# Two products exchanged at the end, and one half of a weighting moved from GpSimd to VectorE, in a one-core attention and FFN kernel

## The chip, the cores and the metric

One core of a Trainium2 chip runs the whole program. The metric is device time in microseconds of one execution. Between executions of the same program the times spread by one to two us (the eleven runs of the old kernel in one call took 342.58 to 344.05), so verdicts are made from several runs of each kernel on the same chip, in rounds that alternate the two. "Span" is the time from the first to the last instruction of the one execution that was profiled; it is some 1.7 us shorter than the device time. A run counts as fast when it is within 1.5% of the fastest of its kernel; only fast runs are compared.

## The reference, cut to what matters

```python
# performer attention, 8 batches x 8 heads x 576 positions x 64; 128 random features
phi(x) = exp(proj - sq - max) / sqrt(m)          # for q and k
kv  = einsum('bhsm,bhsd->bhmd', k_p, v);  z = sum_s k_p
out = (q_p @ kv) / (q_p @ z)
# then a gated FFN on 4608 tokens: 512 -> 1536 -> 512
g = x @ w_gate;  gelu = 0.5 * g * (1 + erf(g / sqrt(2)));  y = (gelu * (x @ w_val)) @ w_out
```

The kernel streams eight batches through attention and then, in blocks of 512 tokens, through the FFN. Two of the FFN's products are made in Strassen's way: seven block products in place of eight, with sums of blocks on VectorE and GpSimd.

## The kernel before: the parts that matter

The program's names, as far as they are needed: `wk` is the scale of k, `kz` the product of k's features with the weighted v, `nd` numerator and denominator of a batch, `pk` the projection of k; `val_one` and `val_two` are accumulators of the FFN's value product. The matmuls of this kernel write to tiles that it calls PSUM tiles (`out_one`, `kz_ps` and the like). In the profile PE is TensorE, DVE VectorE, ACT ScalarE, POOL GpSimd and SP the engine that in this kernel only issues DMAs and waits.

The weighting of v. Each half is one multiplication of 128x1152 elements and one small cast; the kz matmuls read them, the first half of kz only half 0, the second only half 1.

```python
def v(self, half, eng):
    ...
    isl = slice(half * NI // 2, (half + 1) * NI // 2)
    eng.tensor_mul(vev[:, isl, :, :D], vfv[:, isl],
                   wkv[:, isl].unsqueeze(3).broadcast_to((P, NI // 2, 2, D)))
    eng.tensor_copy(vev[:, isl, :, D], wkv[:, isl])
```

Its place in the start of the program (batch 0), in the order in which each engine gets its instructions:

```python
a.w()                       # wk = exp(nmax), ScalarE
a.qt.pe(0)
fill(12)
a.qf(1, True)
a.v(1, pool)                # second half on GpSimd
a.qt.copy(0, dve)
a.v(0, nc.vector)           # first half on VectorE
...
a.kz(0, False)              # reads half 0
a.kz(1)                     # reads half 1
n.qt.copy(0, dve)
n.qt.copy(1, dve)
a.kzc(dve)
```

The last row blocks. `pm` is one of the seven products (six matmuls), `pa` adds a PSUM tile to the output row, `pc` copies one, `pst` stores. Products 1, 6, 7 and 4 of a block are accumulated in one PSUM tile, `out_one`, and read out in between:

```python
def pm(self, s, n, i0, i1):
    ...
    ps = self.two[s][:, 0] if n in (3, 5) else self.two[s][:, 1] if n == 2 else self.one[s]
    for i in range(i0, i1):
        nc.tensor.matmul(ps, x[:, i, s * P:(s + 1) * P], y[:, i], start=n in (1, 2, 5) and i == 0, ...)

def store(c0, o_sb, ns=..., queues=(nc.sync, nc.sync)):
    for i in range(2):      # two DMAs of 64 rows each
        queues[i].dma_start(out=..., in_=o_sb[i * SP:(i + 1) * SP, :])
```

One wait is put in by hand: the DMA transposes of k of batch 2 are held until the load of v of batch 1 has landed.

```python
m = Attention(2)
behind(loads[-2], [m.by_dma("k")])
m.by_dma("q")
```

The softmax here doesn't subtract the row's maximum and nothing guards it: scores larger than these inputs give would overflow.

## Time and profile before

| what | value | from |
|---|---|---|
| device time, median of 3 | 343.06 us (342.66 to 343.08) | the timed runs |
| span of the profiled run | 341.0 us | the page |
| TensorE busy, granted clock | 96%, 0.998 | the page and the view of the cores |
| last copy of the output on VectorE ends | 337.65 us | the timeline |
| from there to the end | 3.3 us | 341.0 - 337.65 |

Reading it: TensorE (PE) is the bound nearly everywhere, so time can only come from the few gaps of PE on the chain, from the head before PE is full, and from the stretch after its last matmul. A timeline row gives start in us, duration in us, engine, line, operation, output and inputs; what stands in brackets at its end is the idle time of that engine ahead of it and what released it. The lines themselves are in the prediction below.

### The profile page before, as it was taken

The numbers are of one execution on the slowest core, as the hardware profiler recorded it, in microseconds if no ns is written. First come the engines' busy times: TensorE is split into PE (matmuls) and PEld (weight loads), VectorE is DVE, ScalarE is ACT, GpSimd is POOL, SyncE is SP. The second block draws the span as 40 slices with busy tenths as digits, with TensorE's granted clock in tenths as the row PEclk, the third lists the DMA queues.
The fourth block names the chain that finished last, engine by engine and source line by source line (L and its number), as shares of the span: only waits on it lengthen the run. The fifth ranks groups of instructions, "written<-read, shape, count | busy, mean of one in ns | idle before, by whom it ended". The sixth has DMA issues, their size and how long they took to land.

```text
span 341.0 us, 7993 instructions
## 1 busy us (share of the span) xinstructions
PE 327.4 (96%) x3114; PEld 206.0 (60%) x3155; DVE 229.1 (67%) x481; ACT 214.3 (63%) x434; POOL 149.9 (44%) x152
## 2 busy tenths in 40 slices
PE   7889999889999999999999999999999999999994
PEld 3565455566646664566447654665466786686683
DVE  3875388979773768375936683677457777796783
ACT  4894366774778558756875677658765447626640
POOL 8326004033486447744674559477968400000000
PEclk9999999999999999999999999999999999999999
DMA  8999999599889256945498629671413040013004
GB/s 155 275 206 207 206 272 206 137 174 236 178 135 331 49 102 91 326 89 108 60 326 113 116 32 291 164 111 19 94 33 63 8 115 11 1 32 93 2 0 124
DMA packets 67173, 45.08 MB, mean 132 GB/s; under 512 B 47296, under 2 KB 60096, under 8 KB 67136
## 3 DMA queue, kind: packets, MB, share of 16 engines
q0 software_dynamic: 14848, 22.12, 31.4%
q1 hardware_dynamic: 51744, 21.64, 30.4%
q10 hardware_dynamic: 544, 0.82, 0.8%
q8 instruction: 24, 0.39, 0.5%
q14 instruction: 13, 0.11, 0.1%
HBM read 37.78 MB, written 9.44 MB: 138 GB/s over the span
## 4 chain that ended last, share of the span: by engine, by line
PE 83%; DVE 6%; DMA 3%; ACT 3%; issue 2%; POOL 2%; DVEq 0%; POOLq 0%
PE g_ps L433 20%; PE o_ps L559 18%; PE val_one L378 11%; PE val_two L378 9%; PE out_one L533 5%; PE out_two L533 3%; PE v_ps L462 3%; PE g_ps L425 3%; PE kz_ps L285 3%; DMA q_in<-in_q_dram 2%; PE nd L302 2%; PE pk L220 2%; DVE x_sb L314 2%; PE pq L242 2%; DVE val_c L387 1%
## 5 line engine op out<-in xcount | busy, mean ns | idle before, releaser
L433 PE MATMUL g_ps<-xT,w_gate_sb 128*128 128x512 bf16 x352 | 108.2, 379 | 0.5
L440 ACT ACTIVATE g_gelu<-g_ps 128x512 bf16<-128x512 f32 x108 | 63.6, 598 | 54.1 <-PE g_ps L433 25.3
L559 PE MATMUL o_ps<-w_out_sb,gated 128*128 128x512 bf16 x275 | 64.6, 380 | 1.1 <-issue 0.6
L480 POOL TENSOR_TENSOR gated<-g_gelu,val_c 128x512 bf16<-128x512 bf16 x29 | 33.7, 1164 | 52.2 <-DVE iden L313 26.3
L387 DVE TENSOR_TENSOR val_c<-val_one,val_c 128x256 f32<-128x256 f32 x48 | 20.3, 424 | 49.0 <-ACT g_gelu L440 40.0
L378 PEld LDWEIGHTS <-w_val_sb 128*128 128x128 bf16 x384 | 36.5, 98 | 17.3 <-issue 1.4
L559 PEld LDWEIGHTS <-gated 128*128 128x128 bf16 x288 | 26.5, 98 | 33.5 <-issue 3.9
L383 ACT COPY val_c<-val_one 128x256 f32<-128x256 f32 x95 | 35.2, 371 | 11.2 <-PE val_one L378 8.1
L378 PEld LDWEIGHTS <-val_sums 128*128 128x128 bf16 x288 | 27.3, 98 | 24.4 <-DVE x_sb L314 3.7
L249 ACT ACTIVATE q_pT<-pq 128x512 bf16<-128x512 f32 (+1 forms) x68 | 34.6, 598 | 11.7 <-PE pq L242 11.5
L233 DVE TENSOR_REDUCE nmax<-pk 128x8 f32<-128x1024 f32 (+2 forms) x43 | 39.7, 968 | 2.9 <-PE pk L220 1.4
L433 PEld LDWEIGHTS <-w_gate_sb 128*128 128x128 bf16 x376 | 34.9, 98 | 11.2
L228 ACT ACTIVATE k_p<-pk 128x1024 bf16<-128x1024 f32 (+2 forms) x43 | 33.0, 832 | 8.1 <-PE pk L220 6.4
L378 PE MATMUL val_one<-x_sums,w_val_sb 128*128 128x256 bf16 x192 | 36.6, 272 | 0.6 <-DVE val_c L387 0.4
L387 DVE TENSOR_TENSOR val_c<-val_two,val_c 128x256 f32<-128x256 f32 x96 | 36.0, 414 | 0.8 <-PE val_two L378 0.7
L271 POOL TENSOR_TENSOR v_ext<-vf,wk 128x1152 bf16<-128x1152 f32 x12 | 28.2, 2347 | 13.9 <-ACT wk L260 13.9
L484 POOL TENSOR_TENSOR gated<-g_gelu,val_c 128x256 bf16<-128x256 bf16 x34 | 24.1, 711 | 15.0 <-ACT g_gelu L440 15.0
L314 DVE TENSOR_TENSOR x_sb<-nd,iden 128x512 bf16<-128x512 f32 (+2 forms) x41 | 27.8, 677 | 1.4
L564 DVE COPY o_sb<-o_ps 128x512 f32<-128x512 f32 x20 | 13.7, 685 | 19.4 <-PE o_ps L559 14.9
L383 ACT COPY val_c<-val_two 128x256 f32<-128x256 f32 x45 | 16.8, 373 | 11.7 <-PE val_two L378 11.7
L484 DVE TENSOR_TENSOR gated<-g_gelu,val_one 128x256 bf16<-128x256 bf16 x48 | 20.0, 416 | 6.0 <-ACT g_gelu L440 5.7
L378 PE MATMUL val_two<-x_sums,val_sums 128*128 128x256 bf16 x96 | 18.4, 274 | 1.0 <-POOL x_sums L455 0.3
(104 smaller groups left out, 486.3 us busy)
## 6 DMA issues: line engine op xcount, KB each, us to landing
out_dram<-o_sb SPq DMA_DIRECT2D x67, 128.0 KB, 3.3
vf<-in_v_dram POOLq DMA_DIRECT2D x7, 1152.0 KB, 12.4
q_in<-in_q_dram POOLq DMA_DIRECT2D x8, 576.0 KB, 9.4
k_in<-in_k_dram POOLq DMA_DIRECT2D x7, 576.0 KB, 6.2
w_gate_sb<-in_moe_w_gate_dram POOLq DMA_DIRECT2D x3, 512.0 KB, 17.7
w_val_sb<-in_moe_w_val_dram POOLq DMA_DIRECT2D x3, 512.0 KB, 19.4
w_out_sb<-in_moe_w_out_dram POOLq DMA_DIRECT2D x3, 512.0 KB, 13.4
vf<-in_v_dram SPq DMA_DIRECT2D x1, 1152.0 KB, 5.7
```

The lines of the kernel that those rows point to most:

```text
L228: last["begun"] = nc.scalar.activation(self.k_p[:, gs, i0:i0 + n, :], pk, func=Exp)
L233: nc.vector.reduce_max(self.nmax[:, gs, i0:i0 + n], pk, axis=AX, negate=True)
L249: last["begun"] = nc.scalar.activation(dst[:, a, i0:i0 + n], self.pq[c][a].rearrange("m (i e p) -> m i e p", e=2, p=SP), func=Exp)
L314: nc.vector.tensor_mul(x_sb[:n].rearrange("p (g h d) -> p g h d", g=2, h=4)[:, gs], ndv[:, :, :, :D], iden[:n, gs].broadcast_to((n, gs.sto ...
L378: nc.tensor.matmul(ps, w[:, c, self.i * P:(self.i + 1) * P], x[:, c], start=first and c == 0, stop=c == 1, skip_group_check=not first)
L383: copy(self.c[:, {1: 0, 6: 1, 5: 2}[n]], self.beta if n == 5 else self.one)
L387: nc.vector.tensor_add(part, (self.gamma, self.beta, self.one)[k], part)
L433: last["begun"] = nc.tensor.matmul(self.gps[jf], w_gate_sb[:, jm, jf * P:(jf + 1) * P], x_tiles[self.t][:, jm], start=(jm == 0), stop=(jm ...
L440: nc.scalar.activation(self.gelus[jf][:, part], src, func=Gelu)
L480: eng.tensor_mul(self.gated[:, i, :], self.gelus[i], self.v[i].row())
L484: eng.tensor_mul(self.gated[:, i + HF, ts], self.gelus[i + HF][:, ts], s.c[:, 2] if half else s.one)
L559: nc.tensor.matmul(self.ps[qq], self.g.gated[:, f, qq * P:(qq + 1) * P], w_out_sb[:, f, :], start=(jf == 0), stop=(jf == N_DFF - 1))
```

## The change

Two independent parts. The first puts both halves of the weighting of batch 0 on VectorE, so that GpSimd's slow instruction (3.32 us there, where VectorE's took 1.36) is out of the way. The second computes the seventh products of the last two row blocks back to back ahead of their fourth products, so that PE has work while VectorE reads a seventh product out of PSUM (twice PE stood idle for 0.52 us there); the last store then goes out whole.

```diff
@@ start of the program
         a.qf(1, True)
-        a.v(1, pool)
+        a.v(1, nc.vector)
         a.qt.copy(0, dve)
         a.v(0, nc.vector)
@@ the last two row blocks
         p.pm(0, 7, 0, HF)
         p.pa(0, 2)
+        p.pm(1, 7, 0, HF)
+        p.pa(1, 2)
         p.pm(0, 4, 0, HF)
         p.pc(0, dve)
         p.pst(0, 1, None, (nc.sync, nc.scalar))
-        p.pm(1, 7, 0, HF)
-        p.pa(1, 2)
-        p.pst(1, 1, 1, (nc.sync, nc.scalar))
         p.pm(1, 4, 0, HF)
         p.pc(1, dve)
-        p.pst(1, 1, 0, (nc.sync, nc.scalar))
+        p.pst(1, 1, None, (nc.sync, nc.scalar))
```

## The prediction

> **What bounds the kernel now.** I read the busy table first: PE 327.4 of 341.0 us, 96%, granted clock 1.00 in all slices. So only a gap of PE on the chain, or the stretch after its last matmul, can give time back. Then I read the chain that ended last, in order of time, in the two stretches that the diff touches.
>
> At the head (batch 0) the chain leaves PE. It runs through the last kx and the scale wk on ScalarE (to 14.65 us), GpSimd's weighting of v, the kz matmuls, kz's copy on VectorE and nd; from 22.7 us on PE is without gaps. These are the timelines of VectorE, GpSimd and PE there (start, duration, instruction, idle before it and its releaser):
> ```profile
> 14.30 0.41 DVE L181 COPY qT<-qT_ps 128x512 bf16<-128x512 bf16 x1
> 14.68 1.36 DVE L271 TENSOR_TENSOR v_ext<-vf,wk 128x1152 bf16<-128x1152 f32 x1
> 15.95 0.23 DVE L273 CAST v_ext<-wk 128x18 bf16<-128x18 f32 x1
> ...
> 14.73 3.32 POOL L271 TENSOR_TENSOR v_ext<-vf,wk 128x1152 bf16<-128x1152 f32 x1 [3.02 <-ACT wk L260]
> 18.01 0.25 POOL L273 CAST v_ext<-wk 128x18 bf16<-128x18 f32 x1
> ...
> 17.32 0.75 PE L285 MATMUL kz_ps<-v_ext,k_p 64*128 64x65 bf16 x36
> 18.31 0.76 PE L285 MATMUL kz_ps<-v_ext,k_p 64*128 64x65 bf16 x36 [0.24 <-POOL v_ext L273]
> ```
> The reader sees that the first kz half needs v(0) (VectorE, done 16.2) and starts at 17.32; the second needs v(1) (GpSimd, done 18.26) and waits only 0.24 us for it. So the 3.32 us of GpSimd are almost hidden; at most that 0.24 us is there to win.
>
> At the tail, the timeline:
> ```profile
> 333.06 0.82 PE L533 MATMUL out_one<-w_out_sb,gated 128*128 128x256 bf16 x6
> ...
> 333.92 0.42 DVE L544 TENSOR_TENSOR o_sb<-out_one,o_sb 128x256 f32<-128x256 f32 x1 [0.16 <-PE out_one L533]
> 334.40 0.81 PE L533 MATMUL out_one<-out_sums,gated 128*128 128x256 bf16 x6 [0.52 <-DVE o_sb L544]
> ...
> 335.05 0.82 PE L533 MATMUL out_one<-w_out_sb,gated 128*128 128x256 bf16 x6
> 335.25 0.42 DVE L547 COPY o_sb<-out_one 128x256 f32<-128x256 f32 x1 [0.91 <-PE out_one L533]
> 335.90 0.42 DVE L544 TENSOR_TENSOR o_sb<-out_one,o_sb 128x256 f32<-128x256 f32 x1 [0.23 <-PE out_one L533]
> 336.38 0.81 PE L533 MATMUL out_one<-out_sums,gated 128*128 128x256 bf16 x6 [0.52 <-DVE o_sb L544]
> ...
> 337.23 0.42 DVE L547 COPY o_sb<-out_one 128x256 f32<-128x256 f32 x1 [0.91 <-PE out_one L533]
> ```
> Product 4 is added into the same PSUM tile as product 7, and VectorE has to read product 7 out in between. In the old order PE stands twice for 0.52 us while VectorE does so. After the last copy (337.65) only the last stores and the end of the program remain: 3.3 us to 341.0.
>
> [...] the median of GpSimd's twelve weightings is 2.156 us, this one took 3.32, and the extra 1.17 us end when VectorE's 1.36 us from 14.68 are over (14.73 + 1.17 = 15.90). VectorE came first and paid nothing (all four of its weightings: 1.35 to 1.37). So moving v(1) makes no VectorE instruction faster.
> [...] the last 64 KB stores land 1.9 and 2.2 us after issue[...].
>
> **Part 1, both halves of v on VectorE.** The order listing of both programs shows v(1)'s two instructions on VectorE after the last nmax and ahead of qt.copy(0); v(0) follows that copy. The first kz half needs v(0), which is now the last of the four. The pitch (start to start) of a weighting is 15.95 - 14.68 = 1.27 us. For the back-to-back pair I take the same operations in a later batch, where both halves are already on VectorE:
> ```profile
> 69.31 1.35 DVE L271 TENSOR_TENSOR v_ext<-vf,wk 128x1152 bf16<-128x1152 f32 x1
> 70.58 0.23 DVE L273 CAST v_ext<-wk 128x18 bf16<-128x18 f32 x1
> 70.66 1.35 DVE L271 TENSOR_TENSOR v_ext<-vf,wk 128x1152 bf16<-128x1152 f32 x1
> 71.92 0.23 DVE L273 CAST v_ext<-wk 128x18 bf16<-128x18 f32 x1
> ```
> A cast costs the next one 0.08. So: v(1) starts at 14.68 as wk (14.65) allows, its cast at 15.95, qt.copy(0) at 16.03 (pitch of such a copy about 0.35), v(0) at 16.38, its cast 17.65 to 17.88. VectorE to PE takes 0.05 (19.81 to 19.86 at nd), so kz starts at 17.93 rather than 17.32, and both halves follow without a wait. A half took 0.58 (18.31 to the next matmul at 18.89): 17.93 + 1.16 = 19.09 against 18.89. **Head: +0.20 us.** The 0.24 wait goes, but the first half comes 0.61 later. The late qt.copy(0) moves qf(0) from 16.20 to about 16.5, ahead of kz, at no cost; ScalarE needs it only at 18.1. The second weight load GpSimd issues next (k of batch 2) can go out 4 us earlier, but behind the same weight loads in the same queue; I give it nothing. After kz everything on the chain follows kz, and PE has no slack from 22.7 on, so I let the 0.20 stay to the end.
>
> **Part 2, the tail.** The same matmuls, adds and copies. PE loses two waits of 0.52 less their overlap: in the gapless stretch six matmuls take 0.65 (334.40 to 335.05). New times: the seventh product of block 0 ends 333.89, that of block 1 334.54; block 0's add ends 334.34, so its fourth product starts at 334.40, and block 1's at 335.06 (its add is done by 335.0). The last product ends 335.06 + 0.81 = 335.87 and its copy 336.31, against 337.65: **1.34 us earlier**.
> Not all of this reaches the end. The last store was half wide, because its other half had gone out at 336.36; now one pair of 128 KB goes, issued at 336.36, and 0.66 us behind another full pair (335.70). Exactly such a couple of pairs is in the trace: issued at 333.13 and 333.78, its last landing came 3.1 us after the second issue. So the last landing is now 336.36 + 3.05 = 339.4, against 337.69 + 2.2 = 339.9: 0.5 us. The end of the program reads the store semaphores one by one on SP, some 0.06 us each, and ends 0.9 us after the last (340.06 to 340.97): the same, within 0.1. **Tail: -0.5 us**; the other 0.8 go back to the stores.
>
> **Sum.** +0.20 - 0.5 = -0.3: span 340.7, time 343.06 - 0.3 = **342.75 us**.
>
> **Rivals.** (a) The stores cost what they did before (2.2 us from the issue) and the whole 1.34 arrive: 343.06 + 0.20 - 1.34 = 341.9. [...] Against: the 3.1 us of the earlier full pair, and a DMA share of 0.9 to 1.0 while these pairs move. (b) The stores take it all back: tail 0, 343.3. Only if the first pair landed later than 3.7 us after its issue, which the trace does not show. (c) v without GpSimd wins its 0.24 us of wait: only if the first kz half were not held, which the instruction order contradicts; 342.3. (d) The head's shift is taken up by a later wait on a DMA, for instance for weights: 342.55. The chain from 22.7 to 330 has one short DMA piece (a transpose of x, released by VectorE itself), so I give it little.
>
> **Range and chances.** The runs of before spread over 0.42 us, and either term may be off by 0.3; together some 0.6 to each side: 342.1 to 343.3. A 2% change is 6.9 us, more than the tail and the head stages' gaps together hold, so same 0.98.
>
> **What would show it.** Head: two VectorE weightings around a qT copy, kz in one run of 72 matmuls from about 17.9 without a wait on GpSimd, and kz's copy at about 19.3 (19.11 before). Tail: no PE idle of 0.5 after 333, last copy ending near 336.3, store pairs of 128 KB, the last landing about 3 us after issue, the span's end near 340.7. The prediction is wrong if the last full pair lands within 2.3 us, if kz starts before 17.6, or if a later stage (another buffer order on PE, the weights' arrival) answers the 0.2 us shift with a larger wait.

The sum came to +0.20 - 0.5 = -0.3 us, so 342.75 us, and both terms rest on lengths read from the old kernel's trace.

## The result

The changed kernel takes 342.31 us (median of four runs, 341.64 to 342.42) against 343.07 us for the old one in the same rounds. The ratio is 0.9974, with a 95% interval of 0.9957 to 0.9991. Ratios here are the mean time of one kernel's fast runs over that of the other's of the same rounds, so not quite the ratio of the medians. It is within 2%, and some 0.9 us faster: more than the 0.3 us that was predicted, and inside the stated range. So there is something to find: 0.6 us that the sum did not hold. (This interval alone, 0.3 to 1.5 us, just reaches the forecast; that of the repetition below, 0.4 to 1.3 us, does not.)

The timelines of VectorE and PE in the head of the changed kernel:

```profile
14.41 1.36 DVE L271 TENSOR_TENSOR v_ext<-vf,wk 128x1152 bf16<-128x1152 f32 x1 [0.30 <-ACT wk L260]
15.69 0.23 DVE L273 CAST v_ext<-wk 128x18 bf16<-128x18 f32 x1
15.77 0.41 DVE L181 COPY qT<-qT_ps 128x512 bf16<-128x512 bf16 x1
16.10 1.35 DVE L271 TENSOR_TENSOR v_ext<-vf,wk 128x1152 bf16<-128x1152 f32 x1
17.37 0.23 DVE L273 CAST v_ext<-wk 128x18 bf16<-128x18 f32 x1
...
16.24 0.39 PE L242 MATMUL pq<-qT,omegaT 64*128 64x512 bf16 x2 [0.29 <-DVE qT L181]
...
17.74 1.34 PE L285 MATMUL kz_ps<-v_ext,k_p 64*128 64x65 bf16 x72 [0.50 <-DVE v_ext L273]
```

Here the reader sees what was expected of the head: two weightings around a copy, and kz as one run of 72 matmuls that now waits 0.50 us for VectorE. The absolute times are not comparable with those of the old profile, because the first load of q landed 0.9 us sooner in this execution (9.74 against 10.67 us), before any changed instruction. So I count from the start of wk on ScalarE: the last kz matmul starts 4.74 us after it, against 4.47 us before. The head is 0.27 us longer at this point.

The tail of the changed kernel, same columns:

```profile
332.51 1.47 PE L533 MATMUL out_one<-w_out_sb,gated 128*128 128x256 bf16 x12
...
333.37 0.42 DVE L544 TENSOR_TENSOR o_sb<-out_one,o_sb 128x256 f32<-128x256 f32 x1 [0.16 <-PE out_one L533]
333.84 1.47 PE L533 MATMUL out_one<-out_sums,gated 128*128 128x256 bf16 x12
334.02 0.42 DVE L544 TENSOR_TENSOR o_sb<-out_one,o_sb 128x256 f32<-128x256 f32 x1 [0.23 <-PE out_one L533]
334.69 0.42 DVE L547 COPY o_sb<-out_one 128x256 f32<-128x256 f32 x1 [0.25 <-PE out_one L533]
335.35 0.42 DVE L547 COPY o_sb<-out_one 128x256 f32<-128x256 f32 x1 [0.23 <-PE out_one L533]
```

Both PE gaps of 0.52 us are gone: twelve matmuls in a row, twice. From the last group of val_two matmuls (those of x_sums with val_sums) to the end of the last copy it is 12.31 us against 13.64, so 1.33 us were won on PE and VectorE. From the last copy to the end of the program it is 4.08 us against 3.31, so 0.77 of them went to the stores. The tail gains 0.56 us.

There is a third place, at which the prediction did not look. Between the first and the last val_two matmuls, some 255 us of nearly gapless PE work in which no instruction was changed, the old kernel took 255.03 us and the new one 254.73. Aligned instruction by instruction, the two traces part there at two places: by 0.07 us near 114 us and by 0.23 us near 297 us. The second in the old kernel, VectorE's timeline and then PE's:

```profile
297.10 0.42 DVE L387 TENSOR_TENSOR val_c<-val_one,val_c 128x256 f32<-128x256 f32 x1 [1.08 <-ACT g_gelu L440]
...
296.24 0.38 PE L378 MATMUL val_one<-x_sums,w_val_sb 128*128 128x256 bf16 x2
```

and in the changed one:

```profile
296.43 0.42 DVE L387 TENSOR_TENSOR val_c<-val_one,val_c 128x256 f32<-128x256 f32 x1 [0.70 <-ACT g_gelu L440]
...
295.94 0.38 PE L378 MATMUL val_one<-x_sums,w_val_sb 128*128 128x256 bf16 x2
```

The add on VectorE needs the two val_one matmuls. In the changed kernel it starts 0.49 us after their start, in the old one 0.86 us. What it waited for had come in both: in the old trace VectorE's wait is recorded at 296.66 us, and the instruction starts 0.44 us later; in the new one the same pair is 0.07 us apart. PE waits for this add before its next val_one group, which starts 1.34 us after the pair above in the old kernel (297.58 us) and 1.08 us in the changed one (297.02), so it loses most of that.

### The profile page after: what moved, and what is told of

The parts are those of the page before. It is cut to its first block, busy times and chain, and to the rows that moved or that the text cites. A ratio compares the mean times of both kernels' runs of the same rounds, so it can differ in the third digit from the quotient of the medians.

```text
span 339.9 us, 7987 instructions
## 1 busy us (share of the span) xinstructions
PE 326.5 (96%) x3114; PEld 205.8 (61%) x3155; DVE 230.2 (68%) x483; ACT 214.2 (63%) x434; POOL 146.3 (43%) x150
## 4 chain that ended last, share of the span: by engine, by line
PE 84%; DVE 8%; ACT 2%; issue 2%; DMA 2%; POOL 0%; SPq 0%; DVEq 0%; POOLq 0%
PE g_ps L433 21%; PE o_ps L559 18%; PE val_one L378 11%; PE val_two L378 9%; PE out_one L533 5%; PE out_two L533 3%; PE v_ps L462 3%; PE g_ps L425 3%; PE kz_ps L285 3%; PE pk L220 2%; DVE nmax L233 2%; PE nd L302 2%; DVE x_sb L314 2%; PE pq L242 2%; DVE v_ext L271 1%
## 5 line engine op out<-in xcount | busy, mean ns | idle before, releaser
L271 POOL TENSOR_TENSOR v_ext<-vf,wk 128x1152 bf16<-128x1152 f32 x11 | 24.8, 2256 | 10.9 <-ACT wk L260 10.9
```

## The experiments

Theory: the head costs 0.2 to 0.3 us, the tail gives 0.5 us, and the rest of the 0.9 us is chance. Rival 1: the relief of GpSimd is a gain after all, or the change speeds up the middle. Rival 2: a later wait takes up what happens in the head.

Times of all runs, each with the old kernel's:

| run | what | median us | old kernel us | ratio (95%) |
|---|---|---|---|---|
| first result | the change | 342.31 | 343.07 | 0.9974 (0.9957 to 0.9991) |
| after_again | the change | 342.29 | 343.21 | 0.9975 (0.9963 to 0.9988) |
| head_only | v on VectorE only | 343.30 | 343.21 | 1.0003 (0.9990 to 1.0015) |
| tail_only | tail only | 342.85 | 343.21 | 0.9990 (0.9977 to 1.0004) |
| v0_first | change, v(0) ahead of v(1) | 342.36 | 343.21 | 0.9976 (0.9963 to 0.9988) |
| before_again | old kernel against itself | 343.21 | 343.15 | 1.0000 (0.9984 to 1.0015) |
| two_idle | old + 2 idle memsets | 343.32 | 343.15 | 1.0003 (0.9991 to 1.0015) |
| one_idle | old + 1 idle memset | 343.15 | 343.18 | 1.0002 (0.9988 to 1.0017) |
| tail_two_idle | tail only + 2 idle memsets | 342.34 | 343.18 | 0.9976 (0.9964 to 0.9988) |
| split_stores | change, stores in four halves | 342.30 | 343.15 | 0.9972 (0.9959 to 0.9984) |
| best | split_stores + v0_first | 342.19 | 343.15 | 0.9972 (0.9956 to 0.9988) |
| split_last | change, last store in halves | 341.97 | 343.18 | 0.9970 (0.9956 to 0.9984) |
| split_last_again | the same | 342.43 | 343.36 | 0.9975 (0.9962 to 0.9989) |

The intervals are some 0.45 us to each side, so single times can't tell parts of 0.3 us. Lengths of stages within the traces can. All are worked out from starts in the trace: from wk's start to the last kz matmul; from wk's start to the first pk matmul that uses the transposed k of batch 2; from wk's start to the first val_two matmul; from there to the last of the 96 val_two matmuls that take x_sums and val_sums; from there to the end of the last copy; from there to the end. (The expectations count kz to the end of its last matmul, 0.19 us later.) All profiles in it are of fast runs. In two_idle's, PE waited 0.75 us for a load of q ahead of kz, before any instruction that its edit touches, hence its later kz.

| profile of | kz | pk | first val_two | middle | to last copy | to the end |
|---|---|---|---|---|---|---|
| old kernel | 4.47 | 40.27 | 54.57 | 255.03 | 13.64 | 3.31 |
| before_again | 4.46 | 40.82 | 55.30 | 255.03 | 13.65 | 3.30 |
| one_idle | 4.46 | 40.25 | 54.60 | 255.09 | 13.64 | 3.31 |
| two_idle | 4.67 | 40.78 | 55.09 | 254.72 | 13.64 | 3.29 |
| tail_only | 4.47 | 40.30 | 54.78 | 255.06 | 12.31 | 4.05 |
| tail_two_idle | 4.46 | 40.21 | 54.78 | 254.73 | 12.31 | 4.01 |
| head_only | 4.74 | 40.55 | 54.74 | 254.73 | 13.64 | 3.31 |
| changed kernel | 4.74 | 40.48 | 54.58 | 254.73 | 12.31 | 4.08 |
| after_again | 4.74 | 40.48 | 54.77 | 254.73 | 12.31 | 4.09 |
| split_stores | 4.74 | 40.48 | 54.69 | 254.72 | 12.31 | 4.09 |
| split_last_again | 4.74 | 40.61 | 54.74 | 254.71 | 12.31 | 3.60 |
| v0_first | 4.17 | 40.13 | 54.80 | 254.73 | 12.31 | 4.06 |
| best | 4.17 | 39.95 | 54.45 | 254.73 | 12.31 | 4.04 |

### 1. The change again

No edit.

> The changed kernel once more, to see how far its own profiles and times move. Theory (head +0.2, tail -0.5, the rest chance): span nearer 340.5 than the 339.9 of its first profile, 0.7 us (0.2%) faster than before at most; within the trace, the head's kz run again ends 4.9 to 5.0 us after the weight wk starts on ScalarE, and the tail again ends 7.3 us after the first of the last four store pairs is issued. The steps of 0.2 to 0.25 us seen near 65 us (a transpose of x by DMA) and near 297 us (a wait of VectorE) should not come back at the same places with the same size; if they do, the change made them. Rival (the change also shortens the middle): those steps come back and the time is again 0.7 us or more below before.

Measured: 0.9975, as the first time, so it is not chance. Tail and kz are the same to 0.01 us. The step near 297 us came back with its size, and so did the one near 114 us: the middle is again 254.73 us. The change itself shortens the middle. The step near 65 us did not come back in the same way; that one was chance.

### 2. Each part alone

head_only is the old kernel with

```diff
-        a.v(1, pool)
+        a.v(1, nc.vector)
```

> Only the weighting of v of batch 0 moved, v(1) ahead of v(0), tail as before. Theory: kz ends about 4.93 us after wk starts, 0.28 later than before, PE stands about 0.5 us ahead of kz for VectorE; time +0.2 to +0.3 us, 343.3. Rival (taking GpSimd's 3.32 us off is a gain): time -0.2 or lower. Rival (a later wait takes it up): no change.

tail_only is the changed kernel with that line undone.

> Only the last two row blocks reordered, head as before. Theory: last copy 1.3 us earlier, the end 0.5 us earlier (last landing about 3.0 us after its issue instead of 2.2); time 0.5 to 0.6 us below before, so 0.2 below the changed kernel. Rival (the stores give nothing back): 1.3 us below before. Rival (the gain of the change is in the head): no change.

Measured: head_only is the same as the old kernel within its interval, tail_only 0.35 us faster by its mean, with an interval that just takes in no change. The two do not add up to the 0.9 us of both; intervals of 0.45 us to each side leave room for that, but do not explain it. In the traces head_only has kz 0.27 us later, and the short middle of 254.73; tail_only has neither. So the short middle belongs to the part that touches only the first 18 us of the program. The table also shows that head_only's 0.27 us at kz are in the scatter by the first val_two: 54.74 us, inside the 54.57 to 55.30 us of the kernels with the old head.

### 3. Where the gain of the middle comes from

All kernels with the short middle had two more instructions in VectorE's stream ahead of 114 us, and two fewer in GpSimd's. The long gap stood ahead of a certain record of VectorE: counted from 0, with waits, number 575. Is it the instruction, or its place in the stream? First the old kernel again:

> The old kernel against itself: ratio 1.000, its interval is the noise of such a comparison. Theory of the middle (a stall of VectorE at a fixed place of its own instruction stream): the 0.43 us between VectorE's wait and its instruction 575 at about 297 us is there again, to 0.02 us. Rival (chance): it is not there, or elsewhere. From wk's start on ScalarE to the first kz copy on VectorE 4.70 us, as in the first profile; end 4.0 us after the last out_one copy's start, 0.1 either way.

It was there: 0.42 us ahead of record 575, middle 255.03 us. Next, two instructions that do nothing that anything reads:

```diff
         a.nx(4)
+        idle = singles.tile([1, 2], F32)
+        nc.vector.memset(idle[:, 0:1], 0.0)
+        nc.vector.memset(idle[:, 1:2], 0.0)
         load_wo(0)
```

> The old kernel with two one-element memsets on VectorE at about 26 us, where VectorE stands idle for 1.8 us; they do no work that anything reads. Theory (the change gains in the middle because VectorE's stream has two instructions more, so another instruction falls on the place where the stream stalls): the 0.43 us wait at 297 us is gone, the stretch from the first val_two to the last group of 96 is 254.73 us as in all kernels with v on VectorE, not 255.05; time 0.3 us (0.09%) below the old kernel. Rival (GpSimd's two instructions less are what matters, or the position of v): the stall stays, no change in time.

VectorE's timeline in two_idle:

```profile
297.51 0.42 DVE L387 TENSOR_TENSOR val_c<-val_one,val_c 128x256 f32<-128x256 f32 x1 [0.70 <-ACT g_gelu L440]
```

The idle time ahead of the add is 0.70 us as in the changed kernel, not 1.08, and the middle is 254.72 us. v still runs half on GpSimd here, and GpSimd has its two instructions. So it is the place in VectorE's stream. The time itself did not show it: 343.32 us where 342.85 was expected, with a first stage in this profile that was 0.5 us longer than the old kernel's; the interval just reaches 0.9991. head_only, the other run with the short middle and the old tail, has the same ratio, 1.0003. An estimate from both intervals together leaves at most 0.2 us of gain, less than the 0.30 us that their traces have in the middle. So in the times the gain of the middle alone is not shown.

Then one memset in place of two:

> The old kernel with one idle memset on VectorE instead of two. Theory (the stall sits between two fixed numbers of VectorE's instruction stream, ahead of its record 575): with one more, the record there is the wait itself, where VectorE stands idle for an operand anyway, so the 0.43 us are hidden and the middle is again near 254.8 us. Rival (two instructions are needed, or the stall belongs to that instruction): the stall ahead of the val_one add is still there and the middle is 255.03 us.

The theory was half right. In one_idle the gap at 297 us is gone, but another opened at 111 us, VectorE's timeline:

```profile
111.66 0.42 DVE L387 TENSOR_TENSOR val_c<-val_one,val_c 128x256 f32<-128x256 f32 x1 [2.01 <-ACT g_gelu L440]
...
296.79 0.42 DVE L387 TENSOR_TENSOR val_c<-val_one,val_c 128x256 f32<-128x256 f32 x1 [0.70 <-ACT g_gelu L440]
```

The old kernel's line at the first place, with its shorter idle time:

```profile
111.53 0.42 DVE L387 TENSOR_TENSOR val_c<-val_one,val_c 128x256 f32<-128x256 f32 x1 [1.64 <-ACT g_gelu L440]
```

The new gap, 0.43 us between wait and instruction, stands ahead of record 191, and 575 - 191 = 384 = 3 x 128. In the old kernel the instruction at record 191 is another one and starts 0.40 us after its predecessor where the like pair near 297 us takes 0.34: these 0.06 us go with the step of 0.07 us near 114 us. There is a third place, 128 records before: at record 63 one_idle's VectorE pauses too,

```profile
43.92 0.68 DVE L353 TENSOR_TENSOR val_sums<-val_sums,w_val_sb 128x1024 bf16<-128x1024 bf16 x1
44.74 0.69 DVE L466 TENSOR_TENSOR gated<-g_gelu,v_ps 128x512 bf16<-128x512 bf16 x1
```

where in the old kernel the same instruction is record 62:

```profile
44.20 0.68 DVE L353 TENSOR_TENSOR val_sums<-val_sums,w_val_sb 128x1024 bf16<-128x1024 bf16 x1
44.80 0.68 DVE L466 TENSOR_TENSOR gated<-g_gelu,v_ps 128x512 bf16<-128x512 bf16 x1
```

The second instruction starts 0.13 us after the first has ended in one_idle, and 0.08 us before that end in the other twelve profiles of the table. So the gaps stand at records 63, 191 and 575, multiples of 128 apart. (A gap of 0.44 us at 87.6 us, in all profiles, is another thing: it moves with its instruction, which waits there for a second semaphore.) What such a place cost depended on what stood there: 0.42 to 0.44 us between a wait and the instruction right behind it, where 0.07 is usual; 0.21 us at record 63; 0.06 us or nothing where VectorE is still busy with the instruction before (record 191 of the old kernel, record 575 of the changed one); nothing to be seen where it waits for an operand anyway (record 575 of one_idle, record 319 of the old kernel at 177.83 us).

What such a place is, no trace shows. The page lists two DMA queues of kind "instruction", the same in the old and the changed kernel, here the old one's (packets, MB, share):

```profile
q8 instruction: 24, 0.39, 0.5%
q14 instruction: 13, 0.11, 0.1%
```

During the run those of q14 are packets of 8192 bytes, those of q8 of 16384. One of 8192 bytes starts within 0.7 us after record 575 (at 297.75 us for 297.10 in the old kernel, 295.46 for 295.31 in the changed one) and after record 191 of the old kernel (112.60 for 111.94). But record 191 of the changed kernel, at 111.22 us, has its nearest ahead of it, at 110.78, and record 63 of the old kernel, at 45.40 us, has its nearest at 44.38 and 48.27. So a link between gaps and packets is not shown; that the gap's place is fixed in VectorE's stream was shown, by the memsets.

Last, the tail alone with two idle memsets and the old head:

> The old head (v(1) on GpSimd), the new tail, and two idle one-element memsets on VectorE at about 26 us. Theory (the changed kernel gains 0.56 us in the tail and 0.31 us by shifting VectorE's stream, and nothing by the weighting itself): no 0.4 us stall at 297 us, the middle 254.73 us, end 4.05 us after the last copy; time 0.8 us below the old kernel, within 0.3 us of the changed kernel. Rival (GpSimd's relief itself is worth something): 0.3 us above the changed kernel or more.

Measured: ratio 0.9976, where the changed kernel has 0.9974 and 0.9975, and tail_only 0.9990. With the new tail, two memsets stand in for the move of the weighting, and the move of v as such is worth nothing that these runs resolve. One thing does not fit: by their times the short middle gave 0.5 us with the new tail (0.9990 to 0.9976) and nothing with the old one (1.0003, twice). The stages of the traces add up, the times of the parts do not; their intervals are too wide to say whether that is more than scatter, and it stays open.

### 4. What becomes of the head's 0.27 us

v0_first is the changed kernel with

```diff
-        a.v(1, nc.vector)
+        a.v(0, nc.vector)
         a.qt.copy(0, dve)
-        a.v(0, nc.vector)
+        a.v(1, nc.vector)
```

> The changed kernel with v(0) ahead of v(1) on VectorE, so the first kz half has its operand first. Theory: kz's first half starts as before (held by ScalarE's release of the PSUM tile, about 3 us after wk starts), the second follows without a wait, kz ends about 4.5 us after wk starts, 0.4 sooner than in the changed kernel and 0.2 sooner than in the old one; time 0.4 us below the changed kernel. Rival (VectorE's total of 3 us holds both halves whatever the order): no change against the changed kernel.

PE's timeline in v0_first, and a part of the chain of waits, in order of time:

```profile
17.70 1.33 PE L285 MATMUL kz_ps<-v_ext,k_p 64*128 64x65 bf16 x72
...
48.05 6.70 DMA kT<-k_in
54.76 0.05 issue
54.80 0.42 PE pk L220 x8
```

The same part of the chain in the old kernel:

```profile
50.64 4.05 PE o_ps L559 x18
54.69 0.41 PE pk L220 x8
```

The order of the halves did what was said of it, and more: kz no longer waits for VectorE, and its last matmul starts 4.17 us after wk, 0.57 us sooner than in the changed kernel where 0.4 was expected. (ScalarE did not hold it here: it was done at 17.39 us, and kz stood behind PE's own transposes of q.) But the time is the same as the changed kernel's, 0.9976. In this trace PE is now ahead of the load side: pk waits for the transposed k of batch 2, which landed at 54.76 us, so it starts 40.13 us after wk and only 0.35 of the 0.57 us are left. At the first val_two nothing is left (54.80 us against 54.58 and 54.77): the transposes of x of this stage are DMAs too (39 of xT in the old kernel's profile, 2.4 us to landing). In the old kernel's first profile PE and that k arrive within 0.1 us of each other (k landed at 54.64 us and pk started at 54.68), and where the loads were late PE waited for them more (before_again: pk 40.82 us after wk). So over all profiles the 0.27 us at kz shrink to 0.08 at pk (mean 40.52 us in the five profiles with v(1) first, 40.44 in the six with the old head) and drown after that.

This shows how a late load takes up what PE gains or loses, but not that it took up the 0.27 us in the changed kernel. PE brings them to pk whole: its matmul ahead of pk starts 40.17 us after wk in all five profiles with v(1) first, 39.90 in the old kernel's. Beside the four old-head profiles in which k came in time (pk at 40.21 to 40.30), 0.2 to 0.3 us are still there at pk; it is the two with a late k (40.78 and 40.82) that bring the means together. At the first val_two the five (54.58 to 54.77 us) lie within the six (54.57 to 55.30), so there the 0.27 us are no longer resolved. In the first pair of profiles they went near 65 us, where the old kernel's PE waited 0.17 us for a transposed x and the changed one's did not; after_again does not repeat that.

One thing stays open. Without GpSimd's weighting the load of k of batch 2 is issued at 13 to 14 us and not at 18 (13.03 in the changed kernel's first profile, with 21.0 us to landing; 18.14 in the old one's, with 17.0). Whether this makes the load side a little earlier can't be told: its landing, counted from wk, scatters by 0.9 us.

### 5. What the stores take back

A pair of 64 KB stores 1.33 us behind one of the same size took 1.9 and 2.2 us to landing (old kernel), a pair of 128 KB stores 0.66 us behind another of that size 2.3 and 3.0 us (changed kernel).

split_stores is the changed kernel with

```diff
         p.pa(1, 2)
+        p.pst(0, 1, 1, (nc.sync, nc.scalar))
+        p.pst(1, 1, 1, (nc.sync, nc.scalar))
         p.pm(0, 4, 0, HF)
         p.pc(0, dve)
-        p.pst(0, 1, None, (nc.sync, nc.scalar))
+        p.pst(0, 1, 0, (nc.sync, nc.scalar))
         p.pm(1, 4, 0, HF)
         p.pc(1, dve)
-        p.pst(1, 1, None, (nc.sync, nc.scalar))
+        p.pst(1, 1, 0, (nc.sync, nc.scalar))
```

> The changed kernel with the last two rows of stores in halves: the right halves go out right after product 7 is added, the left halves after product 4. Theory (the last full pair waits for the pair before it on the DMA engines): last issue unchanged, its landing about 2.2 us after it instead of 3.0, end 0.7 us earlier than in the changed kernel relative to the last copy; time 0.5 to 0.8 us below the changed kernel, 1.3 below the old one. Rival (fixed cost of a store, or four more issues cost as much): within 0.2 us of the changed kernel.

best is the same with v(0) ahead of v(1).

> Stores in halves and v(0) ahead of v(1) on VectorE. Theory: 0.6 us from the stores and 0.1 to 0.3 from the head (the rest of the 0.57 us that kz gains is taken by the wait for the transposed k of batch 2 at 54.7 us, which is tied to the loads): 0.7 to 0.9 us below the changed kernel, 1.5 below the old. Rival (loads absorb all of the head's gain): as split_stores.

Neither gained what was expected: split_stores 0.9972 and best 0.9972, both 4.0 to 4.1 us from the last copy to the end, like the changed kernel. The bytes were out early, but each store took ScalarE 0.47 to 0.81 us to issue, and with four of them in a row its last was issued at 336.77 us where SP's went at 336.08. It landed 1.9 us later, the last of all, 0.47 us behind SP's. SP then read six more semaphores, 0.06 us each, for this one stands early in its order, and the end came 1.27 us after the last landing, not 1.05 as in the changed kernel. So the last landing now came 1.9 us after its issue, not 3.0 as in the changed kernel, but that issue was itself 0.69 us behind SP's. For best the 0.57 us at kz are again only 0.3 us or less by the first val_two.

split_last splits only the very last row:

```diff
         p.pa(1, 2)
+        p.pst(1, 1, 1, (nc.sync, nc.scalar))
         p.pm(0, 4, 0, HF)
         p.pc(0, dve)
         p.pst(0, 1, None, (nc.sync, nc.scalar))
         p.pm(1, 4, 0, HF)
         p.pc(1, dve)
-        p.pst(1, 1, None, (nc.sync, nc.scalar))
+        p.pst(1, 1, 0, (nc.sync, nc.scalar))
```

> The changed kernel with only the last block's second row of stores in halves, its right half sent after product 7. In the run with four halves ScalarE issued each store in 0.6 to 0.8 us and its last one 0.7 us late. Theory (that issue time ate the gain): with one store pair less ScalarE's last issue is at most 0.2 us late, its landing 2.3 to 2.5 us after, the end 3.7 us after the last copy instead of 4.08; time 0.3 us below the changed kernel. Rival (the bytes in the queue decide): end 4.0 us or more after the last copy.

The profile of this run fell on an execution of 676 us, twice the usual time, left out of the ratio; why it was so I don't know. The other five took 341.91 to 343.02 us. So it was run again:

> The same kernel again, for its profile fell in a run of twice the length (676 us; the other five took 341.9 to 343.0), which says nothing of the tail. Theory (ScalarE's issue time ate the gain of four halves): end 3.7 us after the last copy instead of the 4.08 of the changed kernel, the last landing 2.3 to 2.5 us after its issue; time 1.1 us below the old kernel. Rival (the bytes queued before it decide): end 4.0 us or more after the last copy, time 0.85 below.

From the last copy to the end it is now 3.60 us against 4.09, as foreseen: the stores in the trace of after_again and then of split_last_again, last pair (in the second the line takes in ScalarE's store of the full pair as well):

```profile
DMA to landing us min/median/max: 2.3/2.7/3.0
```

```profile
DMA to landing us min/median/max: 2.2/2.4/2.7
```

The tail gives 0.49 us more in the trace. In the times it is not resolved: the five and five fast runs of split_last average 342.20 us, the nine of the changed kernel 342.27. It is the version that I would keep, for its stage in the trace, not for a proven time.

## Why the prediction was right or wrong

- **Within 2%, and inside the range**: right, 342.31 us in 342.1 to 343.3. The forecast of 342.75 was 0.44 us too high, for two reasons that follow.
- **The head, +0.20 us**: at kz it was right in kind and a little small. The weighting stood as said, kz waited and ran in one piece, and kz came 0.27 us later (0.20 predicted). The step that is not borne out is the sentence "After kz everything on the chain follows kz, and PE has no slack from 22.7 on, so I let the 0.20 stay to the end". PE brought the delay to 54.6 us, but there it meets the transposed k of batch 2, which is on its own course through the loads, and by the first val_two, near 69 us, the delay is inside the scatter of the old kernel's profiles. The chain of the one profile showed PE at pk, for the two arrive within 0.1 us of each other. In the times, tail_two_idle with the old head (0.9976) and the changed kernel (0.9974, 0.9975) are the same. Rival (d), a later wait on a DMA, was given "little" and fits; that such waits take up a difference is shown for v0_first, for the 0.27 us it is argued.
- **GpSimd's relief is worth nothing**: right: beside the new tail two idle memsets do the same for the time as the move. One reading on the way is loose: VectorE's weighting ends at 14.68 + 1.36 = 16.04 us, not at the 15.90 that the text gets for GpSimd's release; the two agree to 0.14 us.
- **The middle, 0**: this was not a term of the sum at all. It measured -0.30 us (255.03 to 254.73), because two more instructions in VectorE's stream put a stall of 0.44 us at a harmless place. In the traces this is the largest piece that was missing; in the times it shows only together with the new tail.
- **The tail, -0.5 us**: right by its steps. Last copy 1.34 us earlier predicted, 1.33 measured; last landing 3.05 us after its issue predicted, 3.0 measured; 0.8 us given back to the stores predicted, 0.77 measured; in sum -0.56. The closeness owes something to luck: the earlier couple of pairs that served as the model landed its last store 3.1 us after its issue in that profile, but 3.1 to 3.7 us in the others; the last pair itself keeps to 2.9 to 3.0 in the five profiles that have it.
- **Rival (a)**, the whole 1.34 us arriving, and **(b)**, nothing of it: both fell in the trace, though rival (a)'s 341.9 us lies nearer to the measured time than its ground deserves (a last landing 2.2 us after its issue, where 3.0 was measured). **Rival (c)**'s 342.3 us is the measured time, by luck: kz came 0.27 us later, not 0.24 sooner.

The sum as measured within the traces is -0.56 (tail) - 0.30 (middle) and 0 for the head, which is not resolved, so -0.86 us; the timed ratios 0.9974 and 0.9975 of 343.1 us are -0.87 us. The sums agree better than the intervals of the times, 0.4 us and more to each side, can vouch for.

## What to carry to other kernels

When the instruction counts of an engine change, even by two, compare the stages that were not touched: here, by the traces, a third of the gain (0.30 of 0.86 us) came from a shift of the instruction stream, and a dummy instruction told it from the change's own merit. A wait taken off ahead of a place where two independent tracks meet (here PE's and the loads') was worth only the smaller lead (in v0_first 0.35 of the 0.57 us at pk), and one profile may show only one of the two tracks on its chain. At the end of this program, work that ended 1.33 us sooner also bunched the last stores, and they took 0.77 us back. Four stores in a row from each queue got the bytes out early and gained nothing; with only the last row split it was 0.49 us in the trace, not resolved in the times.
